# Top-k attention and an MLP on one core: twelve probability tiles turned by TensorE instead of VectorE

## The chip, the core and the metric

The kernel runs on one core of a Trainium2 chip. A core has a matrix engine (TensorE, PE in the profile, with its weight loads as PEld), a vector engine (VectorE, DVE), a scalar engine (ScalarE, ACT), a general engine (GpSimd, POOL) and a queue for transfers (SyncE, SP). They run side by side, each through its own instructions in order, and wait for one another through semaphores. The metric is the device time of one execution in microseconds (us), the median of several runs.

## What is computed

Attention over 8 batches and 8 heads with 576 rows of 64 values, in which each row keeps only its 32 largest scores, followed by a normalised MLP with a residual:

```python
scores = scale * np.matmul(q, k.transpose(0, 1, 3, 2))
kth = np.partition(scores, -top_k, axis=-1)[..., -top_k:-top_k + 1]
scores = np.where(scores >= kth, scores, -1000000000.0)
attn = np.exp(scores - np.max(scores, axis=-1, keepdims=True))
attn = attn / (np.sum(attn, axis=-1, keepdims=True) + 1e-09)
x = np.matmul(attn, v)            # heads side by side: (8, 576, 512)
...
xn = (x - mu) / np.sqrt(var + 1e-06) * g_ln
out = x + np.maximum(xn @ w_ch1, 0.0) @ w_ch2   # 512 -> 2048 -> 512
```

All of it is in float32.

## The kernel before

**Units and jobs.** A *unit* is one tile of query rows for a pair of heads: 128 rows and two heads (a whole unit), or the last 64 rows of both heads together (a rest unit, `qt == 4`). There are 160 units, 128 whole and 32 rest. One, two or three units of a head pair form a *job*, and four jobs, one for each head pair `hp` from 0 to 3, take a block of rows through all heads. Rest units come in runs of four at units 40, 60, 72 and 84, and inside the jobs of three units from unit 88 to 143.

**The main loop** makes one step per unit, n from 0 up. The order of every engine's instructions is written out by hand in it, and nothing reorders them later. In step n:
- TensorE computes the scores of unit n+2 (`scores`, L404) into PSUM tiles of the pool `psps`, which has five tiles of one bank each. A whole unit takes four of them, a rest unit two.
- When a job's group is due (two to four steps after its last unit, `lag`), TensorE multiplies its probabilities with the values (`values`, L632 and L640), into one more tile of the same pool, and later turns the product back (`place`, L677).
- ScalarE scales the thresholds of unit n-1 that VectorE found (`prepare`, L459). ScalarE and GpSimd mask unit n-1 (`mask`: L496 on ScalarE, then L499 on GpSimd) into a buffer `e`, of which there are two. Then ScalarE copies the scores of unit n+2 out of PSUM (`take_scores`, L385) into a buffer `sc`, of which there are five, and later in the step takes the exponential of unit n-1 (`weigh`, L507).
- VectorE finds the 32nd largest score of each row of unit n by rounds of maximum and replace (`halve` L425 and L426, `select` L433, L439 and L447). L439 writes a buffer that GpSimd's check of unit n-2 (`watch`, L466) has to have read.
- The probabilities of unit n-2 are turned, since the product with the values needs the keys on the partitions.

**Two ways to turn a unit.** On TensorE (`turn`): four transposes of 128x128 by the identity for each head (L565) into a PSUM tile, a copy of each tile by ScalarE into the operand `pt` (L577), and one more transpose for the last 64 keys of both heads (`turn_ends`, L599, copied at L609). On VectorE (`move`): two instructions turn blocks of 32x32 (L538) into the unit's own score buffer `sc`. A transfer of 512 KB then sends the blocks to a buffer in HBM (L553), and four of 128 KB each bring them back into `pt` in the right place (L548) in step u+3. The last 64 keys of such a unit still go through TensorE, as L599 of step u+3, into a tile of the scores just computed. The flag `moved` of a unit selects VectorE's way. Before the change 87 of the 128 whole units are moved. `lag` depends on the flag of a job's first unit alone.

**Background work.** The MLP of the blocks of rows that are ready (first product L782, second L821 or L942, whose sums ScalarE copies out of PSUM at L907) is a list of single matmuls, which `fill` hands to TensorE at eight places of a step. `slot` sets how many: the work left up to the next block, spread evenly over the steps until then, whatever a step holds otherwise. In the trace each float32 matmul is two records, so a hidden-layer matmul of 256 columns is two records of L782. Blocks also pass through statistics on VectorE (L705) and a turn on TensorE (L741).

## Time and profile before

| | |
|---|---|
| median of 3 runs | 1592.54 us (1591.92 to 1594.62) |
| profiled execution | 1593.68 us, of which the span of the trace is 1591.9 us |
| mean granted TensorE clock | 0.968 |
| VectorE turns, L538 | 174 of 685 ns, 113.6 us busy |
| TensorE turns, L565 | 456 records, 74.5 us busy |
| ScalarE copies of turned tiles, L577 | 82 of 602 ns |
| ScalarE L496 waiting for PE L599 | 178.4 us in 76 waits |
| VectorE L439 waiting for POOL L466 | 41.3 us in 22 waits |
| VectorE L705 waiting for ACT L654 | 33.1 us in 6 waits |

How to read it: the page gives each engine's busy time and its share of the span, then the span in 40 slices with the busy share of each in tenths. A group's line names the source line, the engine, the operation and what is written from what. A timeline line starts with the time and the length in us, and ends with the idle time of the engine before it and what ended that. A line of busy times by stage has the stretch, its length, and each engine's busy time with the number of instructions, then the granted TensorE clock, the share of the transfer engines and GB/s. A wait line has the waiting instruction, what it waited for, the time in us in total, how often, and the longest.

### The profile page before, as it was taken

What the parts mean: (1) busy time and instruction counts of PE and PEld (TensorE: products, weight loads), DVE (VectorE), ACT (ScalarE), POOL (GpSimd) and SP (SyncE); (2) the same over time, 40 slices, a digit from 0 to 9 for tenths busy, and PEclk for the clock granted to TensorE, in tenths of its full rate; (3) what the DMA queues carried; (4) which work ended last, traced back from release to release, by engine and by line L of the source; (5) the groups of instructions that cost most, each with busy time, mean ns of one, the idle gap of its engine ahead of it and who ended that gap; (6) DMA issues with size and microseconds to landing.
All of it is one profiled execution on the core that took longest, in us unless ns stands there. A gap on an engine that the chain in (4) does not pass through costs nothing. (4 is left out here: it accounts for less than half of the span.)

```text
span 1591.9 us, 27533 instructions
## 1 busy us (share of the span) xinstructions
PE 1478.6 (93%) x8106; PEld 1106.5 (70%) x8106; DVE 1365.4 (86%) x3969; ACT 1085.2 (68%) x3153; POOL 997.5 (63%) x1318
## 2 busy tenths in 40 slices
PE   3578889999999999999999999999999999899997
PEld 2356447567777777777777777777777777688886
DVE  6998998999899998989979999999999999657000
ACT  6878887777677777676777776867767766454421
POOL 5968896647474666656656657575757575527614
PEclk6779989999999999999999999999999999999999
DMA  8423641566637754575643675565675555443511
GB/s 207 125 84 101 156 118 45 147 166 185 176 114 197 193 172 124 160 202 143 200 119 115 180 206 164 151 174 155 186 187 154 169 158 157 139 127 106 140 34 49
DMA packets 381784, 234.21 MB, mean 147 GB/s; under 512 B 262964, under 2 KB 350520, under 8 KB 381624
## 3 DMA queue, kind: packets, MB, share of 16 engines
q1 hardware_dynamic: 376888, 231.76, 52.1%
q8 instruction: 67, 1.10, 0.3%
q10 hardware_dynamic: 4736, 0.59, 0.3%
q14 instruction: 93, 0.76, 0.2%
HBM read 160.43 MB, written 71.83 MB: 146 GB/s over the span
## 5 line engine op out<-in xcount | busy, mean ns | idle before, releaser
L499 POOL TENSOR_TENSOR e<-e,sc 128x576 f32<-128x576 f32 x288 | 413.3, 1454 | 472.9 <-ACT e L496 430.9
L782 PE MATMUL hps<-xT,w 128*128 128x256 f32 x2304 | 539.1, 383 | 2.1 <-ACT xT L744 2.1
L447 DVE MAX8 m<-hi 128x8 f32<-128x296 f32 (+1 forms) x1152 | 471.4, 444 | 1.2
L782 PEld LDWEIGHTS hps<-xT,w 128*128 128x128 f32 x2304 | 426.4, 192 | 65.9 <-issue 11.2
L433 DVE MATCH_REPLACE8 hi<-m,hi 128x288 f32<-128x288 f32 (+1 forms) x864 | 377.2, 441 | 0.0
L496 ACT ACTIVATE e<-sc,m 128x576 f32<-128x576 f32 x288 | 209.3, 769 | 182.0 <-PE scps L599 178.4
L942 PE MATMUL ops<-w,h 128*128 128x256 f32 x1280 | 306.5, 385 | 5.8 <-POOL h L878 3.5
L942 PEld LDWEIGHTS ops<-w,h 128*128 128x128 f32 x1280 | 237.4, 193 | 40.7 <-issue 5.0
L507 ACT ACTIVATE e<-e,m 128x576 f32<-128x576 f32 x288 | 225.4, 785 | 24.5 <-POOL e L499 21.8
L385 ACT COPY sc<-scps 128x288 f32<-128x288 f32 x576 | 187.2, 402 | 42.8 <-POOL e L499 32.5
L439 DVE MAX8 hi<-lo 128x8 f32<-128x288 f32 x288 | 117.8, 444 | 41.3 <-POOL watched L466 41.3
L632 PE MATMUL av<-pt,vb 128*64 128x256 f32 (+2 forms) x1280 | 144.6, 368 | 0.5 <-ACT e L507 0.5
L538 DVE STREAM_TRANSPOSE sc<-e 128x512 f32<-128x512 f32 x174 | 113.6, 685 | 34.6 <-ACT e L507 28.7
L805 ACT ACTIVATE h<-hps 128x512 f32<-128x512 f32 x144 | 87.2, 606 | 77.4 <-PE hps L782 76.9
L425 DVE TENSOR_TENSOR hi<-sc 128x576 f32<-128x576 f32 (+1 forms) x160 | 133.2, 833 | 3.0 <-ACT sc L385 3.0
L426 DVE TENSOR_TENSOR lo<-sc 128x576 f32<-128x576 f32 (+1 forms) x160 | 133.5, 835 | 0.0
L404 PE MATMUL scps<-kT,late_qT 64*128 64x288 f32 (+3 forms) x832 | 122.7, 413 | 0.2 <-ACT pt L577 0.2
L565 PE MATMUL tp<-ident,e 128*128 128x128 f32 x456 | 74.5, 291 | 50.3 <-ACT e L507 30.8
L942 PE MATMUL ops<-wt,s 128*128 128x256 f32 x512 | 118.4, 380 | 0.6 <-POOL s L872 0.6
L632 PEld LDWEIGHTS av<-pt,vb 128*64 128x64 f32 x1280 | 78.3, 138 | 57.5 <-issue 15.6
L404 PE MATMUL scps<-kT,qT 64*128 64x288 f32 x512 | 94.4, 467 | 22.7 <-DVE qT L331 11.2
L565 PEld LDWEIGHTS tp<-ident,e 128*128 128x128 f32 x456 | 57.5, 148 | 77.1 <-ACT e L507 37.5
(107 smaller groups left out, 1910.0 us busy)
## 6 DMA issues: line engine op xcount, KB each, us to landing
turned<-sc SPq DMA_DIRECT2D x87, 512.0 KB, 3.8
pt<-turned SPq DMA_DIRECT2D x348, 128.0 KB, 2.8
w<-forms SPq DMA_DIRECT2D x128, 256.0 KB, 4.6
vb<-in_v_dram SPq DMA_DIRECT2D x80, 288.0 KB, 4.1
raw<-in_moe_w_ch_dram SPq DMA_DIRECT2D x32, 512.0 KB, 4.7
kT<-kept SPq DMA_DIRECT2D x48, 288.0 KB, 3.5
kin<-in_k_dram SPq DMA_DIRECT2D x128, 72.0 KB, 2.7
kept<-kT SPq DMA_DIRECT2D x32, 288.0 KB, 3.2
```

The costliest lines, as they stand in the source:

```text
L385: nc.scalar.copy(u.sc[:, t, s * HALF : (s + 1) * HALF], u.made[s][t][:, 0:HALF])
L404: nc.tensor.matmul(ps[i * R : i * R + ql, o : o + width], qT[r, q0 : q0 + ql], kT[r, k0 : k0 + width], start=True, stop=True,)
L425: nc.vector.tensor_tensor(hi, a, b, ALU.max)
L426: nc.vector.tensor_tensor(lo, a, b, ALU.min)
L433: nc.vector.match_replace(x, m[:, t, :], x, LOWEST)
L447: nc.vector.max(m[:, t, :], u.hi[:, t, 0:width])
L496: nc.scalar.activation(u.e[:, t], u.sc[:, t], AF.Relu, bias=u.edge[:, t : t + 1], scale=-STEEP)
L499: nc.gpsimd.tensor_tensor(u.e[:, t], u.e[:, t], u.sc[:, t], ALU.subtract)
L507: nc.scalar.activation(u.e[:, t], u.e[:, t], AF.Exp, bias=u.bias[:, t : t + 1], scale=-scale, accum_out=g.den[:, col : col + 1],)
L632: nc.tensor.matmul(av[h * D : (h + 1) * D, 0 : g.nq], vb[:, h * (J + 1) + c, :], g.blocks[:, h, 0 : g.nq // 32, c, :], start=(c == 0), sto ...
L782: nc.tensor.matmul(ps[0][:, side * N : (side + 1) * N], w1[:, c, f * P : (f + 1) * P], self.xT[:, c, 0:N], start=(c == 0), stop=(c == NC - 1),
L942: nc.tensor.matmul(bank[name][:, 0:Q], a(j), rhs, start=first and j == 0, stop=(j == G - 1), skip_group_check=not first,)
```

## The change

One condition in the loop that sets `moved` changes. A unit that is not its job's last is moved as before. The last unit of a job was moved where the next job does not start with a rest unit, and the job is of a batch above 1 with an even `hp`, or the unit is one of the last 19. Now the even `hp` no longer counts: of last units, only those of the last 19 are moved.

```diff
         for u in units[max(j.first, EARLY) : j.last + 1]:
             u.moved = not u.rest and u.i >= jobs[3 * NHP].first and (
                 u.i < j.last
-                or (j.b > 1 and (j.hp % 2 == 0 or u.i > N - 20))
+                or u.i > N - 20
                 and nj is not None and not units[nj.first].rest
             )
```

The flag changes for twelve units: 33, 37, 45, 49, 53, 57, 65, 69, 77, 81, 101 and 105, each the second unit of a job of two. They are turned on TensorE in steps 35, 39, 47, 51, 55, 59, 67, 71, 79, 83, 103 and 107, and 75 units are left to VectorE. No job's `lag` changes, and `slot` deals out the background matmuls as before. In each of these steps `turn` puts four L565 after three background matmuls (in step 79 after one and the eight transposes L741), four more some matmuls later, and L599 after these. L599 of the same unit, one step later, is gone, and so are the L538 pair, the L553 transfer and the four L548 transfers. Since a unit that is not moved has no further use of its `sc` buffer after L499, the buffers of the later units rotate differently. In most of the steps u+3 the copy L385 waited for a buffer that GpSimd's L499 of that step had read, and it now waits for one whose transfer to HBM is over.

## The prediction

> **What bounds the kernel now.** I read the page's busy shares first, then its slices, then the busy times by stage, and last the waits and the instruction timeline of the engines that wait. A *step* here is one pass of the main loop: VectorE searches unit n, TensorE computes the scores of unit n+2 and turns unit n-2. I bound a step on VectorE by the starts of L425 and on TensorE by the starts of the scores (L404).

> ```profile
> PE 1478.6 (93%) x8106; PEld 1106.5 (70%) x8106; DVE 1365.4 (86%) x3969; ACT 1085.2 (68%) x3153; POOL 997.5 (63%) x1318
> PE   3578889999999999999999999999999999899997
> DVE  6998998999899998989979999999999999657000
> ```

> The page shows two engines near full. In the last sixth VectorE has little left and TensorE works off the rest alone. The busy times by stage (columns PE, PEld, DVE, ACT, POOL) say which engine leads where the twelve units lie:

> ```profile
> 348.27:411.10 62.83, 60.92 (x354) 45.46 (x354) 62.76 (x191) 44.67 (x135) 44.81 (x62) 1.00 0.64 182
> 411.10:453.61 42.51, 42.51 (x280) 33.34 (x279) 35.41 (x109) 30.90 (x101) 20.98 (x33) 1.00 0.50 138
> 453.61:575.97 122.36, 116.58 (x683) 89.00 (x683) 119.32 (x358) 88.52 (x260) 76.92 (x109) 1.00 0.66 181
> 575.97:627.95 51.98, 51.98 (x354) 40.36 (x348) 45.57 (x139) 39.31 (x124) 26.93 (x38) 1.00 0.50 146
> ```

> They alternate. In the pair steps (rows 1 and 3) VectorE is without a gap but for 3.0 us, and TensorE lacks 1.9 and 5.8 us. In the steps of 64-row rest units (rows 2 and 4) VectorE idles 7.1 and 6.4 us and TensorE not at all: a rest step is short on VectorE, but the background matmuls are dealt out by step, so TensorE falls behind. So the end of each such group is set by when TensorE entered it, and what counts is whether TensorE was late because of VectorE or of itself. Its own waits tell:

> ```profile
> PE tp L565 <- ACT sc L385: 3.8, 3, 2.1
> PE xo L677 <- ACT oT L650: 1.5, 2, 0.9
> PE av L632 <- ACT e L507: 0.5, 1, 0.5
> ```

> That is all from 453.61 to 575.97 us: TensorE waits for ScalarE's evacuation of PSUM. How such a wait arises is seen in the timeline of TensorE, then of ScalarE, in step 37, which already turns a unit on TensorE:

> ```profile
> 386.78 0.33 PE L599 MATMUL scps<-ident,e 128*128 128x128 f32 x1
> 386.94 1.46 PE L942 MATMUL ops<-w,h 128*128 128x256 f32 x6
> 389.28 0.66 PE L565 MATMUL tp<-ident,e 128*128 128x128 f32 x4 [0.88 <-ACT sc L385]
> 389.77 1.46 PE L942 MATMUL ops<-w,h 128*128 128x256 f32 x6
> ...
> 387.20 1.44 ACT L496 ACTIVATE e<-sc,m 128x576 f32<-128x576 f32 x2 [0.77 <-PE scps L599]
> 388.55 1.27 ACT L385 COPY sc<-scps 128x288 f32<-128x288 f32 x4
> ```

> ScalarE's mask (L496) waits for the end-turn L599, since that is the last reader of the e buffer; only then come the copies L385 that free a score bank, and the transposes L565 need one. TensorE bridges this with six background records (0.214 us each from start to start) and stands still for the rest. The 0.88 us recurs at 489.35, 525.47, 665.48 and 767.24 us, wherever VectorE stands: it is a fixed chain, not a late VectorE.

> [...] a background record shows 0.383 us on average, at a pitch of 0.214. [...] The kernel's pools take 5 + 3; a whole unit's scores take four of the five and the values product the fifth, and the gap of 0.88 us fits. [...] a wait of 2.08 us at 561.38 us left the rate whole.

> **The change part by part.**

> *Removed from VectorE:* per unit two L538, 1.29 us together (at 508.09 us, x2). Twelve: 15.5 us of busy time. Also 12 sends of 512 KB and 48 fetches of 128 KB on SP's queue; no wait above is for them, so I cost this at nothing.

> *Added on TensorE:* eight L565 in step u+2. Four take 0.43 us (392.16 to 392.59), so 0.86 us; L599 (0.11 us) only moves one step ahead. With them comes the wait of step 37: 389.28 - 386.94 less six records is 1.05 us lost. The changed steps have the same order: scores, values, L599 of the unit before, three background matmuls, L565. So 1.9 us on TensorE where four score banks are held (steps 35, 47, 51, 55, 67, 79, 103, 107), but 0.86 in steps 39, 59, 71, 83, where the scores are of a rest unit and take two banks. What is late today in these steps is xo L677 waiting for oT; as TensorE comes later, that is absorbed: 0.6 (35), 0.3 (39), 1.1 (51), 0.7 (55), 0.5 (83), 0.7 (103), 0.2 us (107), counted from start to start as above, which is 0.17 us more than the idle time shown. In step 79 the x transposes already pay the PSUM wait (1.74 us), so only 0.9 is added. Bounds of the added wait: none (if ScalarE's copies come early), or 1.05.

> *Added on ScalarE:* two copies L577 of 0.60 us per unit, 14.5 us in all; hidden behind its 32% idle, except where they queue ahead of the exponential, as in step 37 today. Taken as nothing; at worst 1.2 us a unit.

> *Freed on ScalarE:* in step u+3 the score copy goes today into a buffer whose last reader is GpSimd's L499 of the same step. In the changed program the send's buffer takes its place. The wait is about 2.2 us each; it mostly falls into slack, but not at 654.73 us:

> ```profile
> 652.93 1.46 PE L942 MATMUL ops<-wt,s 128*128 128x256 f32 x6
> 656.37 2.92 PE L942 MATMUL ops<-w,h 128*128 128x256 f32 x6 [1.97 <-ACT o L907]
> ...
> 654.73 1.31 ACT L385 COPY sc<-scps 128x288 f32<-128x288 f32 x4 [2.80 <-POOL e L499]
> ```

> Here TensorE loses 1.97 us and then runs six records in 2.92 instead of 1.46, and scores in 1.52 instead of 1.24: 3.7 us that the change should give back (bounds 0 and 3.7).

> *The sum, as TensorE's arrival at the end of each stretch* (VectorE, sooner, only waits longer there):
> - to 453.6: steps 35 (0.86 + 1.05 - 0.6 = 1.3) and 39 (0.6): +1.9.
> - to 628: steps 47 (1.9), 51 (0.8), 55 (1.2), 59 (0.9) = 4.8. VectorE is 3 x 1.29 = 3.9 us sooner by step 57, so what TensorE waits for it goes: 2.08 - 0.88 at 561.38 and 0.7 at 520.65, 1.9 us. +2.9.
> - to 714: steps 67 (1.9), 71 (0.9), less 3.7: -0.9.
> - to 843: steps 79 (0.9), 83 (0.4): +1.3.
> - to 1325: VectorE has 4.0 us idle in step 90 and then leads, so here its 2 x 1.29 = 2.6 us (steps 103, 107) count, while TensorE comes about 2.1 us later (1.2 + 1.7, less about 0.8 of waits that go). From step 111 on the two are level (1012 to 1325: TensorE idles 1.9 us in four waits), so TensorE's lateness takes back most of it. Bounds -2.6 and +2.1; taken as 0.

> Sum: 1.9 + 2.9 - 0.9 + 1.3 + 0 = +5.2 us. The tail after 1325 us has unchanged work and only shifts. The profiled execution took 1593.7 us (span 1591.9), so 1598.9; it lies 1.1 us above the median of 1592.54, from which I forecast 1597.7 us.

> **Rivals.**
> 1. *VectorE's time reaches the end (faster).* For it: VectorE has no gap in 122.36 us but 3.0, and TensorE lacks 5.8 us there. Against it: a pair of steps whose second unit is turned on TensorE takes it 6.6 + 11.2 = 17.8 us (scores at 547.57 to 554.18, and at 383.30 to 394.53), as long as VectorE's 10.2 + 7.7 = 17.9 (L425 at 492.73 to 502.90, and at 484.99 to 492.73). It decides where TensorE enters the rest steps with waits for VectorE left. Full: 1592.5 - 15.5 = 1577; half of it: 1585.
> 2. *No new PSUM wait.* ScalarE, freed from the buffer wait, copies in time: seven waits of about 1.05 go, of which the absorbed L677 waits keep half. +5.2 - 4 = about +1: 1593.5, no change.
> 3. *ScalarE pays too.* The added copies delay the exponentials by up to 1.2 us in half the steps and the return at 656 us fails: 5.2 + 3.7 + 4 = +13: 1605.

> That the change does not do what it says is excluded: the order of instructions has 24 fewer L538 and 96 more L565.

> **How the numbers follow.** Forecast 0.60 (1593 to 1602), rival 1 0.22, rival 2 0.12, rival 3 0.06. A difference of 0.2%, 3.2 us, is about what can be told from none. Faster: rival 1, 0.22. Same: rival 2 and the low edge of the forecast, 0.15. Slower: 0.63. The range goes from the better half of rival 1 to just past the forecast's upper edge: 1585 to 1603.

> **What would show it.** Right: VectorE's busy time falls by about 15 us but its idle time grows by about 20; L538 x150 and L565 x552; the wait of L565 for L385 grows by six or seven times 0.88 us, on steps 35, 47, 51, 55, 67, 103, 107; TensorE stays without idle time through the rest steps and enters them later; the 2.2 us waits of L385 for L499 are gone, and so is the gap at 656 us. Wrong: TensorE enters the rest steps sooner, or has waits for VectorE's thresholds (through L459) before them; or L565 waits no more often than now.

## The result and the profile after

| | median | runs | lowest to highest |
|---|---|---|---|
| before | 1592.91 us | 6 | 1590.85 to 1594.62 |
| after | 1599.76 us | 6 | 1599.07 to 1602.59 |

The ratio is 1.0047 [1.0034, 1.006] (in brackets its 95% interval): 6.85 us slower, where the forecast was 5.2 us slower (1597.7). The span of the profiled execution went from 1591.9 to 1597.9 us. One of the 36 runs of the kernel before that stand beside experiments 4 to 6 took 5215.62 us and counts in none of their medians and ratios.

The page of the changed kernel first: the busy shares, then the slices of TensorE and VectorE.

```profile
PE 1487.4 (93%) x8202; PEld 1115.2 (70%) x8202; DVE 1369.6 (86%) x3945; ACT 1098.4 (69%) x3177; POOL 1014.3 (63%) x1318
...
PE   3578889999999999999999999999999999999997
...
DVE  6997998999899997989978999999999999658100
```

TensorE has its 96 added transposes (8106 to 8202 instructions). VectorE has 24 instructions fewer, and yet it is busy 4.2 us *more* (1365.4 before). The groups of the page by line show where its freed time went:

```profile
L426 DVE TENSOR_TENSOR lo<-sc 128x576 f32<-128x576 f32 (+1 forms) x160 | 148.8, 930 | 0.0
...
L425 DVE TENSOR_TENSOR hi<-sc 128x576 f32<-128x576 f32 (+1 forms) x160 | 136.7, 854 | 3.0 <-ACT sc L385 3.0
L538 DVE STREAM_TRANSPOSE sc<-e 128x512 f32<-128x512 f32 x150 | 98.4, 686 | 34.2 <-ACT e L507 28.4
```

L538 gave 15.2 us back (113.6 to 98.4). L425 and L426, whose number and size are unchanged, took 3.5 and 15.3 us more (133.2 and 133.5 before): the same work, recorded as longer. Experiment 7, below, measures such a lengthening by itself (0.72 to 1.32 us).

Next, the busy times by stage, for the four stretches of steps that the prediction showed (steps 33, 40, 46, 59 and 66 begin them, by VectorE):

```profile
348.89:410.27 61.38, 59.18 (x348) 44.36 (x347) 61.31 (x188) 42.89 (x127) 44.08 (x60) 1.00 0.55 154
410.27:456.18 45.91, 45.91 (x302) 36.15 (x301) 38.00 (x109) 34.72 (x113) 23.41 (x36) 1.00 0.44 125
456.18:578.67 122.49, 117.22 (x687) 89.48 (x687) 119.45 (x352) 91.02 (x266) 84.13 (x109) 1.00 0.57 155
578.67:634.10 55.43, 55.43 (x381) 42.95 (x380) 45.12 (x137) 40.75 (x127) 27.55 (x38) 1.00 0.41 118
```

The steps of rest units (rows 2 and 4) have grown from 42.51 to 45.91 and from 51.98 to 55.43 us, with TensorE full as before and VectorE's idle time up from 7.1 to 7.9 and from 6.4 to 10.3 us. The pair steps (rows 1 and 3) are 1.45 us shorter and 0.13 us longer. Counted from step 33, VectorE reaches the first group of rest steps 1.45 us sooner and TensorE 1.99 us later; the second group VectorE reaches 2.08 us later, since it has waited in the first, and TensorE 4.34. In both VectorE waits longer for a TensorE that comes later.

TensorE's waits, as a total of the whole run (the time, how often, the longest), and how one looks in a changed step, on TensorE and then on ScalarE:

```profile
PE tp L565 <- ACT sc L385: 24.1, 24, 2.1
```

```profile
473.44 0.33 PE L599 MATMUL scps<-ident,e 128*128 128x128 f32 x1
473.60 1.46 PE L942 MATMUL ops<-w,h 128*128 128x256 f32 x6
475.94 0.66 PE L565 MATMUL tp<-ident,e 128*128 128x128 f32 x4 [0.88 <-ACT sc L385]
...
473.86 1.44 ACT L496 ACTIVATE e<-sc,m 128x576 f32<-128x576 f32 x2 [1.75 <-PE scps L599]
475.21 1.28 ACT L385 COPY sc<-scps 128x288 f32<-128x288 f32 x4
```

This is step 47, the chain of step 37 over again: L599, then the mask L496, then the copy L385 that gives a score bank back, and only then L565. Before, there were 17 such waits; the seven new ones are in steps 35, 47, 51, 55, 67, 103 and 107, each of 0.88 us. None is in steps 39, 59, 71 or 83. The total grew by less than seven times 0.88, because two old waits became shorter: in step 57 from 2.08 to 0.88 us, in step 105 from 1.22 to 0.88.

The gap near 656 us is gone. Here is TensorE at the same place, with the copy on ScalarE:

```profile
654.99 1.89 PE L942 MATMUL ops<-wt,s 128*128 128x256 f32 x8
656.81 1.24 PE L404 MATMUL scps<-kT,late_qT 64*128 64x288 f32 x8
657.98 2.86 PE L942 MATMUL ops<-wt,s 128*128 128x256 f32 x12
660.68 0.27 PE L684 MATMUL xo<-ident,oTr 128*128 128x128 f32 x1
...
657.70 1.39 ACT L385 COPY sc<-scps 128x288 f32<-128x288 f32 x4
```

L385 follows the mask at once, where it waited 2.80 us for GpSimd's L499, and twelve background records run at full rate (2.86 us, at a granted clock of 1.00). L385's idle time fell from 42.8 to 14.7 us over the run.

### The profile page after: what moved, and what is told of

The parts are those of the page before. It is cut to its first block, busy times and chain, and to the rows that moved or that the text cites. A ratio compares the mean times of both kernels' runs of the same rounds, so it can differ in the third digit from the quotient of the medians.

```text
span 1597.9 us, 27656 instructions
## 1 busy us (share of the span) xinstructions
PE 1487.4 (93%) x8202; PEld 1115.2 (70%) x8202; DVE 1369.6 (86%) x3945; ACT 1098.4 (69%) x3177; POOL 1014.3 (63%) x1318
## 5 line engine op out<-in xcount | busy, mean ns | idle before, releaser
L499 POOL TENSOR_TENSOR e<-e,sc 128x576 f32<-128x576 f32 x288 | 416.0, 1464 | 469.2 <-ACT e L496 432.8
L496 ACT ACTIVATE e<-sc,m 128x576 f32<-128x576 f32 x288 | 209.3, 769 | 206.6 <-PE scps L599 202.7
L942 PE MATMUL ops<-w,h 128*128 128x256 f32 x1280 | 307.2, 384 | 3.5 <-POOL h L878 3.5
L942 PEld LDWEIGHTS ops<-w,h 128*128 128x128 f32 x1280 | 235.8, 193 | 38.4 <-issue 6.2
L507 ACT ACTIVATE e<-e,m 128x576 f32<-128x576 f32 x288 | 225.3, 784 | 26.2 <-POOL e L499 23.6
L385 ACT COPY sc<-scps 128x288 f32<-128x288 f32 x576 | 187.3, 401 | 14.7 <-PE scps L404 6.4
L439 DVE MAX8 hi<-lo 128x8 f32<-128x288 f32 x288 | 117.8, 444 | 44.1 <-POOL watched L466 44.1
L426 DVE TENSOR_TENSOR lo<-sc 128x576 f32<-128x576 f32 (+1 forms) x160 | 148.8, 930 | 0.0
L632 PE MATMUL av<-pt,vb 128*64 128x256 f32 (+2 forms) x1280 | 145.3, 369 | 0.0
L565 PE MATMUL tp<-ident,e 128*128 128x128 f32 x552 | 89.3, 288 | 55.4 <-ACT e L507 31.3
L425 DVE TENSOR_TENSOR hi<-sc 128x576 f32<-128x576 f32 (+1 forms) x160 | 136.7, 854 | 3.0 <-ACT sc L385 3.0
L565 PEld LDWEIGHTS tp<-ident,e 128*128 128x128 f32 x552 | 69.0, 147 | 86.1 <-ACT e L507 37.5
L538 DVE STREAM_TRANSPOSE sc<-e 128x512 f32<-128x512 f32 x150 | 98.4, 686 | 34.2 <-ACT e L507 28.4
L404 PE MATMUL scps<-kT,late_qT 64*128 64x288 f32 (+3 forms) x832 | 121.4, 409 | 0.3 <-ACT pt L577 0.2
L942 PE MATMUL ops<-wt,s 128*128 128x256 f32 x512 | 119.5, 381 | 0.7 <-POOL s L872 0.7
L632 PEld LDWEIGHTS av<-pt,vb 128*64 128x64 f32 x1280 | 78.4, 139 | 57.8 <-issue 15.4
L404 PE MATMUL scps<-kT,qT 64*128 64x288 f32 x512 | 95.0, 469 | 22.8 <-DVE qT L331 10.7
```

The costliest lines, as they stand in the source:

```text
L385: nc.scalar.copy(u.sc[:, t, s * HALF : (s + 1) * HALF], u.made[s][t][:, 0:HALF])
L404: nc.tensor.matmul(ps[i * R : i * R + ql, o : o + width], qT[r, q0 : q0 + ql], kT[r, k0 : k0 + width], start=True, stop=True,)
L426: nc.vector.tensor_tensor(lo, a, b, ALU.min)
L496: nc.scalar.activation(u.e[:, t], u.sc[:, t], AF.Relu, bias=u.edge[:, t : t + 1], scale=-STEEP)
L499: nc.gpsimd.tensor_tensor(u.e[:, t], u.e[:, t], u.sc[:, t], ALU.subtract)
L507: nc.scalar.activation(u.e[:, t], u.e[:, t], AF.Exp, bias=u.bias[:, t : t + 1], scale=-scale, accum_out=g.den[:, col : col + 1],)
```

## The experiments

The theory: TensorE sets the end, the twelve units cost it their transposes and the wait for a score bank, and VectorE's freed time is worth nothing while that price stands. The rivals: VectorE's time counts, or the price lies elsewhere (ScalarE, transfers). Where a step is called sooner or later, the start of its scores on TensorE is compared with the profile of the kernel before, counted from step 33 if nothing else is said. Each median stands beside that of the kernel before from the same chip.

**1. Give VectorE's time back as empty work.** The changed kernel, with three MAX8 (VectorE's search for the eight largest values) of unused result on VectorE where each of the twelve turns stood:

```diff
         if moved:
             move(ex)
+        elif ex and ex.i in CHANGED:
+            for r in range(3):
+                spent = brief_small.tile([P, 8], FP32, tag="spent", name="spent")
+                nc.vector.max(spent[:], u.hi[:, 0, 0:HALF])
```

> The changed kernel with three further MAX8 of 288 columns (about 0.44 us each) on VectorE in each of the twelve steps, at the place where L538 stood: VectorE gets back its 15.5 us, TensorE keeps the transposes. If TensorE sets the pace and VectorE's freed time was worth nothing (my theory), the time stays within 2 us of the changed kernel's 1599.8, and VectorE's waits (L439 for L466) and the stretched part of L425 and L426 shrink by what is added. If VectorE's time reaches the end, it is 12 to 16 us slower, about 1613.

Measured: 1600.11 us, before 1593.21, ratio 1.0038 [1.0025, 1.0051]; the changed kernel had 1.0047. By TensorE's scores the profile of the changed kernel and this one have the same lengths: 122.24 and 122.23 us from step 33 to 47, 86.57 and 86.58 from 66 to 76, 186.13 and 186.13 from 103 to 125. VectorE's 36 added MAX8 (15.8 us) do not move the end, and VectorE is not even busy for longer (1369.0 us, 1369.6 in the changed kernel): L425 gives back 2.1 us, and the time of L426 falls from 148.8 to

```profile
L426 DVE TENSOR_TENSOR lo<-sc 128x576 f32<-128x576 f32 (+1 forms) x160 | 136.8, 855 | 0.0
```

So in the changed kernel this much of VectorE's time, at these places, is worth nothing.

**2. Leave the turns out.** The changed kernel, but for the twelve units ScalarE copies the probabilities unturned into the operand of the product, and the eight L565 are left out; what is multiplied with the values is then not the turned tile.

```diff
         def part(t):
+            if u.i in CHANGED:
+                nc.scalar.copy(
+                    g.blocks[:, t, i0 : i0 + P // 32],
+                    u.e[:, t, 0:JP].rearrange("p (c i n) -> p i c n", c=J, n=32),
+                )
+                return
             ps = turned()
```

> The changed kernel without the eight transposes L565 of each of the twelve units: ScalarE copies the unturned probabilities into the operand, as many and as large copies as before, so the products of these units are not the reference's. Neither VectorE nor TensorE turns them. Against the kernel before this shows what VectorE's 15.5 us are worth when TensorE pays nothing. My theory: the wait for VectorE before step 58 (1.9 us), the gap at 656 us (3.7 us) and 0 to 2.6 us after 843 us go, 6 to 8 us faster than before, about 1586. If VectorE's time counts in full: 15 us faster, about 1577. Against the changed kernel it gives TensorE's price, 12 to 15 us.

Measured: 1586.19 us, before 1593.21, ratio 0.9952 [0.9939, 0.9965]. That is 7.0 us under the kernel before and 13.6 under the changed one. With no price on TensorE, the relief of VectorE, ScalarE's buffer and the transfers is worth 7 us: by step 70 the scores are 5.1 us sooner (the gap at 656 us and 1.4 us of waits before it), and from step 90 to 149 another 0.9. A further 1.6 us lie behind TensorE's last multiplication (experiment 5). ScalarE does the same number of copies as in the changed kernel, so ScalarE's added work is not the price.

**3. The order of L565, with and without the change.** If the 0.88 us come from the score bank, the first four L565 cost nothing once they stand behind more background matmuls. In both kernels they are handed out later, behind the first exponential of unit n-1. ScalarE's copy of their tile (L577) moves with them, behind that exponential:

```diff
-        if parts:
+        later_turn = len(parts) > 2 and n > CONVERTING
+        if parts and not later_turn:
             parts[0]()
...
         if mk and mk.i >= EARLY:
             weigh(mk, 0)
+        if later_turn:
+            parts[0]()
```

The changed kernel with it:

> The changed kernel with the first four transposes of a unit handed to TensorE about two to three background matmuls later, behind the ones that fill the wait for PSUM; nothing else moves. If the fixed chain L599, L496, L385 makes the 1.05 us wait (my theory), it goes in the steps that have it, after the change some fourteen, and the time falls by 5 to 12 us below the changed kernel, to about 1591; where oT is late, the wait shows at L677 instead. If the wait is for something else, the time stays at 1599.8.

and the kernel before with it:

> The kernel before with the same later place of the first four transposes. The wait of 1.05 us goes in steps 33, 37, 49, 53, 57, 69, 81, 105 and 109, of which four or five lie where TensorE leads: 3 to 5 us faster than before, about 1588.5. If the wait is for something else: no change, 1592.9.

Measured: 1587.59 us, ratio 0.9963 [0.9949, 0.9977], and 1588.13 us, ratio 0.9964 [0.995, 0.9977], both beside 1593.21. Here is step 37 of the first:

```profile
387.25 0.33 PE L599 MATMUL scps<-ident,e 128*128 128x128 f32 x1
387.42 2.76 PE L942 MATMUL ops<-w,h 128*128 128x256 f32 x12
390.01 0.60 PE L565 MATMUL tp<-ident,e 128*128 128x128 f32 x4
```

Twelve background records instead of six bridge the chain, and L565 no longer waits. Over the run its waits for L385 fall from 24.1 to 7.9 us:

```profile
PE tp L565 <- ACT sc L385: 7.9, 5, 2.2
```

Two things follow. The wait is one of order: 12 us of the changed kernel hang on where four transposes and their copy stand. In the profiles step 149 comes 11.5 us sooner than in the changed kernel, and TensorE's idle time between the scores of steps 33 and 149 falls from 19.1 to 8.1 us, so it is the waits on TensorE that pay, hardly the copy. And with that order the twelve units cost nothing that the medians show: 1587.59 against 1588.13 us, whose intervals overlap almost wholly. Most of what the transposes take is balanced by shorter waits (TensorE idles 8.1 us against 16.0 in the same steps), but not all: step 149 comes 1.4 us later with the twelve units than without them, and what evens it out lies behind the last multiplication (experiment 5).

**4. The one unit that should pay.** By the sum of the prediction unit 65 alone is worth its transposes and wait, 1.9 us, against the 3.7 us gap that its freed buffer removes. The kernel before, with

```diff
+    for i in (65,):
+        units[i].moved = False
```

> The kernel before with unit 65 alone turned on TensorE (step 67). My theory: TensorE pays 1.9 us in step 67, and the buffer wait of L385 for L499 in step 68 goes with the 1.97 us gap and the half-rate records behind it, 3.7 us: TensorE reaches the end of the rest steps after it 1.8 us sooner, about 1591.3. If the gap near 656 us has another cause, or comes back at a later place, TensorE is 1.9 us later: about 1595.

Measured: 1590.33 us (22 runs), before 1593.51 (35), ratio 0.9981 [0.9972, 0.9989]. TensorE in its trace:

```profile
644.74 0.65 PE L565 MATMUL tp<-ident,e 128*128 128x128 f32 x4 [0.88 <-ACT sc L385]
...
648.37 1.89 PE L942 MATMUL ops<-wt,s 128*128 128x256 f32 x8
650.19 1.24 PE L404 MATMUL scps<-kT,late_qT 64*128 64x288 f32 x8
651.36 2.86 PE L942 MATMUL ops<-wt,s 128*128 128x256 f32 x12
```

The new wait is there, and the gap that the kernel before had at 656 us is not. Counted from step 66, the scores are 2.09 us later at step 68 and 1.86 sooner by step 70: the size that the prediction's two terms gave (1.9 - 3.7). But part of the second term is chance. Of the four profiles in which L385 still waits here, all have the gap on TensorE (1.97 to 2.00 us), and only two the half rate behind it (before, where the granted clock is 0.50 from 656.41 to 659.82 us, and the first run of experiment 5); in the other two (the kernel before with the later order, of experiment 3, and the second run of experiment 5) step 70 comes 1.6 us sooner than in before, again from step 66, with unit 65 as it was. So of the 3.95 us that come back between steps 68 and 70 some 2.3 are certain, about what unit 65 pays, and 1.6 come only where the half rate does. Of the 3.2 us by which the medians differ, 1.6 lie behind the last multiplication (experiment 5).

**5. The last stretch.** The prediction put the effect after step 90 at nothing. The kernel before with units 101 and 105 alone (the same two lines, with `(101, 105)`):

> The kernel before with units 101 and 105 alone turned on TensorE (steps 103 and 107). Forecast term 0, from a VectorE that leads there. If TensorE leads there too, as the traces of the changed kernel and of the one without the transposes say (1.85 us later, and only 0.85 us sooner): about 1.9 us slower than before, 1595, and VectorE comes as late as TensorE by step 123. If VectorE leads: 0 to 2.6 us faster.

Measured: 1593.13 us (14 runs), before 1593.51, ratio 0.9998 [0.999, 1.0006]. In the trace the last stretch was 1.86 us longer, and the total no longer, so it was run again:

> The kernel before with units 101 and 105 turned on TensorE, a second time, since the first gave +1.86 us in the trace's last stretch and nothing in the total. If TensorE's 1.86 us reaches the end: before + 1.5 to 2.3 us. If the tail takes it back: before within 0.6 us. In the trace the scores of step 149 start, counted from the scores of step 90, 1.86 us later than in the kernel before, either way.

Measured: 1592.74 us (13 runs), before 1594.02 (17), ratio 0.9994 [0.9985, 1.0002]. The busy times of the last stretch (steps 90 to 149, by TensorE's scores), of before, of after, and of this run:

```profile
841.07:1320.82 479.75, 473.75 (x2603) 357.72 (x2602) 477.15 (x1398) 346.31 (x1049) 306.55 (x429) 1.00 0.60 169
```

```profile
847.31:1328.92 481.61, 475.06 (x2619) 359.10 (x2618) 478.42 (x1394) 348.51 (x1053) 312.14 (x429) 1.00 0.58 164
```

```profile
842.31:1323.89 481.58, 475.05 (x2620) 359.10 (x2619) 478.40 (x1394) 348.16 (x1053) 312.31 (x429) 1.00 0.58 164
```

The stretch is 1.86 us longer in after and 1.83 here: two units' price on TensorE, not set off by VectorE's 2.6 us. Two things keep it out of the total. One is seen in two steps of the tail, first of before, then of this run (the third number from the end is TensorE's granted clock):

```profile
1320.82:1342.96 22.14, 18.88 (x97) 14.59 (x96) 22.00 (x64) 11.95 (x36) 9.19 (x14) 0.92 0.59 170
1383.07:1404.89 21.82, 18.36 (x88) 14.12 (x87) 10.84 (x35) 8.15 (x25) 6.89 (x12) 0.84 0.48 144
```

```profile
1323.89:1344.72 20.83, 17.38 (x96) 13.64 (x96) 20.69 (x61) 11.94 (x36) 9.20 (x14) 1.00 0.61 167
1384.84:1405.44 20.60, 17.14 (x88) 13.15 (x87) 10.83 (x35) 8.15 (x25) 6.89 (x12) 0.92 0.50 152
```

Both kernels have the same gaps of 3.0 and 3.5 us on TensorE here, and after them the granted clock is 0.50 for 10.2 us in all in the profile of before, and for about 3.3 us in this (an estimate from the last line: 0.08 x 20.60 / 0.5). 2.5 us come from that, in work that the edit doesn't touch; it varies between executions of one program (in the first run the granted clock was 0.97 over the 120 us from 1300 us on, so an estimate of 7 us at 0.50).

The other is the same in both runs, and stands behind everything else: SyncE's last waits, after the output is sent (in total, how often, the longest), first of before from 1587 us on, then of after from 1595 us on:

```profile
SPq L1411 <- SPq L1411: 4.1, 2, 2.6
```

```profile
SPq L1411 <- SPq L1411: 2.5, 1, 2.5
```

The second wait, of 1.5 us, is in the two profiles with all 87 moved units (before, and before with the later order) and in none of the eight with fewer. From TensorE's last multiplication to the end it makes 11.4 and 11.5 us there, and 9.7 to 9.9 in the others. So by the profiles every change of flags here gains some 1.6 us at the end, whatever it does in the loop; why SyncE then waits once instead of twice isn't shown. With it the medians fit the traces: 1.86 us lost in the stretch and about 1.5 gained at the end leave 0.3 us, which the first interval (up to 1.0 us) holds and the second (up to 0.3) has at its edge. How long the clock is low comes on top of this, and varies from one execution to the next.

**6. Both gains together.** The kernel before, with the order of experiment 3 and unit 65 turned on TensorE:

> The kernel before with the later place of the first transposes and unit 65 turned on TensorE: what the runs so far point to. Theory: the 5 us of the later place, and of unit 65 the return of the gap at 656 us less the price of its transposes (3.7 - 0.9): about 1585.5, 2 to 3 us below the later place alone. Otherwise about 1588 as without unit 65.

Measured: 1584.89 us (7 runs), before 1593.51, ratio 0.9948 [0.9929, 0.9967]. It has the lowest median of all, under both kernels. That it beats the order alone (1588.13) isn't certain: the two intervals overlap, and the gain behind the last multiplication is part of the difference.

**7. L425 and L426 by themselves.** A kernel of its own, which leaves the reference's whole computation out: VectorE operations of this kernel's sizes, alone and beside GpSimd.

```diff
+    def two():
+        nc.vector.tensor_tensor(c[:], a[:], b[:], ALU.max)
+    def gp_two():
+        nc.gpsimd.tensor_tensor(k[:], g[:], h[:], ALU.subtract)
+    def gp_one():
+        nc.gpsimd.tensor_scalar(k[:], g[:], 1.0, 0.5, ALU.mult, ALU.add)
```

> A kernel of its own that computes nothing of the reference: groups of VectorE operations of the sizes used here, each group once alone, once beside GpSimd subtractions of two operands (128x576), once beside GpSimd operations of one operand. Theory [...]: the maximum of two operands takes about 0.75 us alone and 1.2 to 2 us on average beside the GpSimd subtractions, while MAX8 and replace over 288 values stay at about 0.44 us and the 512-value turn at about 0.69, each within 5%. Rival A (both engines slow each other whatever they read): all four VectorE operations get longer beside GpSimd. Rival B (the long L425 and L426 wait for data, not for GpSimd): none of the four changes.

Its timeline where GpSimd begins its subtractions (L31 is the maximum of two operands, L40 the turn of 512 values, L43 the subtraction):

```profile
35.55 0.74 DVE L31 TENSOR_TENSOR c<-a,b 128x576 f32<-128x576 f32 x1
35.79 5.51 POOL L43 TENSOR_TENSOR k<-g,h 128x576 f32<-128x576 f32 x3 [0.66 <-DVE g L50]
36.22 0.70 DVE L40 STREAM_TRANSPOSE e<-e 128x512 f32<-128x512 f32 x1
36.84 1.33 DVE L31 TENSOR_TENSOR c<-a,b 128x576 f32<-128x576 f32 x1
38.10 0.70 DVE L40 STREAM_TRANSPOSE e<-e 128x512 f32<-128x512 f32 x1
38.72 1.32 DVE L31 TENSOR_TENSOR c<-a,b 128x576 f32<-128x576 f32 x1
```

The maximum of two operands goes from 0.72 to 1.32 us, and the turn between stays at 0.70. Measured over the whole run, in us, as the median (number):

| VectorE operation | alone | beside GpSimd, two operands | beside GpSimd, one operand |
|---|---|---|---|
| maximum of two, 128x576 | 0.716 (39) | 1.322 (13) | 0.716 (20) |
| MAX8, 288 values | 0.461 (41) | 0.461 (36) | 0.461 (31) |
| replace, 288 values | 0.442 (8) | 0.442 (32) | 0.442 (50) |
| turn, 512 values | 0.701 (40) | 0.698 (12) | 0.700 (20) |

So it is neither a slowing of everything nor a wait for data: of these operations only the form with two operands pays, and only beside GpSimd's form with two operands. GpSimd pays as well: its subtraction takes 1.40 us beside the other VectorE operations, and 1.80 here. GpSimd's form with one operand does leave VectorE alone, but goes from 0.67 to 1.18 us itself beside the maxima and turns. In the full kernel the line is not so sharp: six L425 and L426 of before lie beside nothing but GpSimd's L164, which has one operand, and take 0.30 us longer on average.

## Why the prediction was right, and where it was not

**What bounds, and the wait.** That TensorE leads in the stretches up to step 90, that a rest step passes on TensorE's lateness, and that a unit turned on TensorE brings the wait of step 37 with it held (experiments 1 and 3). The seven steps named for the wait are the seven in which it appeared, at the length named.

**The sum.** Each stretch by TensorE's arrival, from the profile:

| stretch, to | forecast | measured |
|---|---|---|
| 348.7 us (step 33) | 0 | +0.6 |
| 453.6 us | +1.9 | +1.93 |
| 628 us | +2.9 | +3.27 |
| 714 us | -0.9 | -1.00 |
| 843 us | +1.3 | +1.41 |
| 1325 us | 0 | +1.86 |
| end (tail) | 0 | -2.1 |

The four terms from step 33 to 843 us are within 0.4 us. That the absorbed waits of L677 and VectorE's lead in the pair steps had to be taken off is what made them fit. The return of the gap at 656 us was taken at its upper bound; that the profile of before had the half rate there, which two of four have, is luck (experiment 4).

The terms also show what the price is made of. Between the scores of steps 33 and 149 TensorE idles no longer after the change (19.1 us) than before (20.2), and yet takes 7.5 us more. The 96 transposes take 10.3 us (0.107 us each, as the prediction has it); less the 1.1 us of idle time and the 1.7 us of the half rate at 656 us, that is an estimate of 7.5. The seven new waits took the place of others that went: 2.8 us for L677, 2.3 for L942, 1.5 in steps 57 and 105.

**The term that failed** is "to 1325": "VectorE has 4.0 us idle in step 90 and then leads, so here its 2 x 1.29 = 2.6 us (steps 103, 107) count". They did not count: the stretch came out 1.86 us longer with all twelve units and 1.83 to 1.86 with those two alone, near the upper bound of 2.1, and experiment 2 gained only 0.9 us there with VectorE's relief and no price. The step that failed is reading a VectorE without gaps as the leading engine. In that stretch of the kernel before, VectorE lacked 2.6 us and TensorE 6.0. TensorE's waits there (the total, how often, the longest) are:

```profile
PE xo L677 <- ACT oT L650: 3.5, 6, 1.1
PE tp L565 <- ACT sc L385: 2.1, 2, 1.2
PE ops L942 <- ACT o L907: 0.3, 1, 0.3
```

All are for ScalarE's copies. A late VectorE can stand behind such a wait, as behind the 2.08 us at 561.38; here at most 0.34 us are of that kind, by which one wait of L565 exceeds 0.88. And VectorE's busy time was longer here than its operations take by themselves: its 43 L426 of 576 values took 5.1 us more there than the 0.748 us that each takes where no GpSimd instruction lies beside it, and its 43 L425 took 5.8 us more than 0.737. These 10.9 us of its 477.15 are little as a share, but four times VectorE's idle time of 2.6 us.

A related mistake made another line of the prediction wrong: VectorE's busy time was to fall by about 15 us and its idle time to grow by about 20. Busy time grew by 4.2 and idle time (span less busy) by 1.8, from 226.5 to 228.3. The slack that VectorE gained turned into longer L425 and L426 (18.8 us), not into idle time.

**The tail** "has unchanged work and only shifts", says the prediction. It changed by -2.1 us, of which 0.5 lie on TensorE and 1.6 behind its last multiplication (experiment 5). That happens to cancel the missed term, so the sum came out nearer than its parts: it is luck that the forecast of 5.2 us lies so near the 6.0 us between the two profiles and the 6.85 between the medians.

**The rivals.** Rival 1, VectorE's time reaching the end, fails in the changed kernel (experiment 1); it is true only of a kernel without the price (experiment 2), and there the 7 us still include up to 3.7 of the gap that ScalarE's freed buffer removes and 1.6 behind the last multiplication. Rival 2, no new wait, fails with the seven waits. Rival 3, ScalarE paying too, is excluded by the gap that did go, and by experiment 2 with the same copies.

## What to carry to other kernels

An engine without gaps need not lead: ask of its operations whether they take as long as the same form does where nothing runs beside it (here L426 takes 0.75 us without a GpSimd instruction beside it, and up to 1.97 in the profile of before), and test the lead by adding empty work to it. Work moved between two full engines is priced by its own time and by the wait that it meets at its new place, and here the order of four transposes was worth more (12 us in the changed kernel, 5 in the one before) than which engine made them. A change of twelve places is a sum of gains and losses by stretch, and the end of the program is one of them: before a difference of medians is put down to a term of the loop, see whether the profiles agree from the last multiplication on.

## What was not expected of the hardware

**The same work recorded as longer.** In this kernel L426 with 576 values takes 0.742 to 0.756 us where no GpSimd instruction lies beside it (44 in before). The longest, which have GpSimd's instructions beside them for over 1.2 us, take 1.9 us on average (10 in before, 17 in after). One of after, from the timelines of VectorE and GpSimd:

```profile
1018.10 0.86 DVE L425 TENSOR_TENSOR hi<-sc 128x576 f32<-128x576 f32 x1
1018.89 1.96 DVE L426 TENSOR_TENSOR lo<-sc 128x576 f32<-128x576 f32 x1
1020.77 0.80 DVE L447 MAX8 m<-hi 128x8 f32<-128x288 f32 x2
...
1016.93 3.30 POOL L499 TENSOR_TENSOR e<-e,sc 128x576 f32<-128x576 f32 x2 [4.28 <-ACT e L496]
```

L426 ends 0.6 us after GpSimd's two L499, 1.2 us late, with no idle time shown. In experiment 7 the maximum of two operands went from 0.72 to 1.32 us beside GpSimd's subtractions of two operands, and stayed at 0.72 beside its operations of one operand. That this is the whole cause of the 1.9 us here is not shown, since no VectorE operation of experiment 7 took longer than 1.33. What makes the two engines slower side by side is not shown either.
